# One level of Strassen's method in block 0's first product for two chunks, a new order of the weights, and a weight's sign made by ScalarE

## The chip, the core and the metric

The kernel runs on one core of a Trainium2 chip (trn2). The core has TensorE (PE; PEld is its weight load) for matmuls, VectorE (DVE), ScalarE (ACT) and GpSimd (POOL) for element-wise work, and SyncE (SP), whose queue issues most of the DMA transfers here. Matmuls read SBUF and write PSUM, which has eight banks; VectorE and ScalarE read PSUM and SBUF. The engines run side by side, each one in the order of its own queue, and wait for one another by semaphores.

The metric is the device time of one execution in microseconds. A profile is one further execution, taken apart: "span" runs from its first instruction to its last.

## What is computed

```python
kv  = einsum('bhsd,bhse->bhde', k, v)              # 8 batches, 8 heads, 576 rows, 64 columns
out = einsum('bhsd,bhde->bhse', q, kv)
x   = out / sqrt(mean(out**2, -1) + 1e-6) * g_norm # then heads side by side: 4608 x 512
h   = x @ w_in                                     # 512 x 2048
g   = maximum(0.01 * h, h)
y   = g @ w_out                                    # 2048 x 512
```

The kernel reads all inputs as they are given: `w_in` and `w_out` come as 64-bit floats, which no engine computes with, and are rounded to 32 bits on the chip.

## The kernel before

**Blocks and chunks.** The 4608 rows of `x` are cut into nine blocks of 512 (`NB`, `NT`), and the 2048 columns of `w_in` into four chunks of two halves (`h`) of two strips (`u`) of 128 columns (`NC`, `U`). Blocks 1 to 8 form both products by Strassen's method, with one level or two. Block 0 runs while the weights are still arriving, and forms them plainly, in `first_block`.

**A plain step of block 0.** For strip n = 0 to 15 an h group of four matmuls (128 rows of weight, 512 columns of `x`) fills a PSUM bank (`h_ps`, banks ha and hc in turn); ScalarE's Prelu (L1313) writes it to SBUF as `gT`. One step later an o group multiplies `gT` by the strip's two rows of `w_out` into four banks (`o_acc`: oa, oc, hb, hd), in which all sixteen strips add up. After each half step `between(n, half)` is called: it takes one step of block 1's attention (kv groups, transposes of q on VectorE, o_ps groups, the norm), where `steps` has one for that call, and lets some more weights be loaded and rounded.

**A weight.** There are 32 jobs (`w_jobs`): 16 of `w_in`, each of four DMAs of 128 KB, and 16 of `w_out`, each one DMA of 512 KB. In the list they take turns. A job's 512 KB land in one of seven homes (in `stage` and `pairs`, `raw_homes`), so job j + 7 can only be loaded when job j has been read. SP's queue also carries the loads of k, v and q for blocks 1 and 2 at fixed places between the jobs. `round_f64` turns 64 bits into 32: ScalarE reads the low word (`add`, L264) and the high word (`cut`, L262) into temporaries; VectorE clamps `cut` (L266), shifts it left by three (L271), sets the sign bit from it (L273) and adds the two (L278). Where the job's home is in two pieces (`w2_1`, "apart"), shift and sign go to a third temporary (`high`), and the last addition is made in two. Four temporaries with two buffers each (`spare`) go round. All these steps are pinned in program order on their engines.

**Strassen's method, one level.** `strassen(tags, left, right, done)` runs seven products in the order 1, 2, 6, 5, 7, 3, 4 (`ORDER`). A product is four matmuls of 256 columns: two of 128 rows each for two pieces of the result. Products 1, 6, 7, 4 add up in the first bank of `tags`, 2, 5, 3 in the second; 1, 2 and 5 start a bank afresh. After a product `done` is called. In `product_h`, for one chunk of h, it copies the banks after products 1, 5 and 6 to SBUF (ScalarE, L904 and its like), adds the bank to such a copy after 2, 3 and 7 (VectorE, `add`, L669) with a Prelu behind it (`relu`, L864), and after 4 takes a Prelu straight from the bank. Sums of quarters of the weights come from `sides_w1` (GpSimd, into the homes `pair(0)` and `pair(1)`), sums of quarters of `x` from `sides_x` (VectorE).

**Behind block 0.** VectorE and ScalarE copy the four `o_acc` banks to `o_all`, and ScalarE's queue issues the stores. Then block 1 begins: its first h group needs only `x` and the rounded weights, its third the first sums. GpSimd's sums for block 1 start during block 0, as soon as the homes in `pairs` that they are written to have been read for the last time; two one-element copies hold it there until the last weight is rounded.

A scheduler puts unpinned instructions in their place on each engine; matmuls and what is passed to `pin` keep the program's order.

Of the kernel before, what the change touches and what calls it, by code (L numbers as in the profile page):

```python
# [9 lines left out]

F32 = mybir.dt.float32
U32 = mybir.dt.uint32
I64 = mybir.dt.int64
AF = mybir.ActivationFunctionType
AX = mybir.AxisListType
ALU = mybir.AluOpType
# [8 lines left out]
def kernel(  # L25
# [91 lines left out]
    def pair(i, *shape):  # L117
        return view(pairs, i * NW, *shape)

    def matmul(*args, **kw):  # L120
        pin(nc.tensor.matmul(*args, **kw))  # L121
# [94 lines left out]
    def w2_rows(h, c, u):  # L216
        return w2_1[:, :, c, u, :] if h else w2_0[c][:, u:u + 1, :]
# [4 lines left out]
    def spare(n, name, dtype=F32):  # L222

        return gpool.tile([P, n], dtype, tag=next(spare_homes), name=name)
# [61 lines left out]
                w_jobs += [(w1_sb[h][c][:, u], w_in_e[:, :, :, f0:f0 + P]),  # L286
                           (w2_rows(h, c, u), w_out[f0:f0 + P].rearrange("p (v n) -> p v n", v=1 + h))]

    w_jobs[1:-1] = [w_jobs[i + 1 if i % 2 else i - 1] for i in range(1, len(w_jobs) - 1)]
    w_raws = {}  # L290
    halved = [j for j, (_, src) in enumerate(w_jobs) if src.shape[1:] == (2, N2)]

# [12 lines left out]
    def round_w(j):  # L305
        for _ in rounding(j):
            pass

    eps_sb = consts.tile([P, 1], F32, name="eps_sb")
    nc.vector.memset(eps_sb, EPS)  # L310
# [357 lines left out]
    def add(eng, out_, a, b_, minus=False, pinned=False):  # L668
        ins = eng.tensor_tensor(out_, a, b_, op=ALU.subtract if minus else ALU.add)  # L669
        if pinned or steady:  # L670
            pin(ins)

    def sides_w1(c):


        a11, a12 = w1_sb[0][c][:, :, :2, :], w1_sb[0][c][:, :, 2:, :]
        a21, a22 = w1_sb[1][c][:, :, :2, :], w1_sb[1][c][:, :, 2:, :]
        s12 = pair(0, U, 2, 2, P)
        sides = {1: a11, 2: a12, 4: a22, 5: s12[:, :, :, 0, :], 6: s12[:, :, :, 1, :]}
        add(nc.gpsimd, sides[5], a21, a22)  # L680
        add(nc.gpsimd, sides[6], sides[5], a11, True)

        def more():
            s34 = pair(1, U, 2, 2, P)
            sides.update({7: s34[:, :, :, 0, :], 3: s34[:, :, :, 1, :]})
            add(nc.gpsimd, sides[7], a11, a21, True)
            add(nc.gpsimd, sides[3], a12, sides[6], True)
        return sides, more

    w2_dram = [[dram.tile([P, 2, U, N2], F32, name=f"w2_{c}_{i}") for i in range(2)]  # L690
# [134 lines left out]
    def strassen(tags, left, right, done, order=ORDER, pieces=None):  # L825

        banks = {}
        for i in order:  # L830

            if i is None:
                yield
                continue
            b = tags[0 if i in (1, 6, 7, 4) else 1]
            if i in FRESH:
                banks[b] = ps_m.tile([P, 2, N2], F32, tag=b, name=f"{b[0]}_{b[1]}")
            bank = banks[b]
# [41 lines left out]
    def sums_of(c, to):  # L880

        g11, g21, g22, g12 = g_of(c)
        s1, s2, s3, s4 = (gpool.tile([P, 4, P], F32, tag=f"gs{i}", name=f"gs{i}")
                          for i in range(1, 5))
        to.update({1: g11, 2: g12, 3: s4, 4: g22, 5: s1, 6: s2, 7: s3})
        last_s4[c] = s4
        eng = nc.gpsimd if c < END - 1 else nc.vector
        if c == END - 1:
            yield
        add(eng, s1, g21, g22)  # L890
        add(eng, s2, s1, g11, True)
        if c == END - 1:
            yield
        add(eng, s3, g11, g21, True)
        add(eng, s4, g12, s2, True)

    def product_h(c, w_sides, x_sides, to):

        g11, g21, g22, g12 = g_of(c)

        def done(i, bank):

            if i == 1:
                nc.scalar.copy(g11, bank)  # L904
            elif i == 5:
                nc.scalar.copy(g22, bank)
            elif i == 2:
                add(nc.vector, g11, bank, g11, pinned=True)
                relu(g11)
            elif i == 6:  # L910
                nc.scalar.copy(g21, bank)
            elif i == 3:
                add(nc.vector, g21, bank, g21, pinned=True)
                relu(g21)
            elif i == 7:
                add(nc.vector, g22, bank, g22, pinned=True)
                relu(g22)
            else:
                relu(g12, bank)

        yield from strassen((("ha", "hc"), ("hb", "hd"))[c % 2], lambda i, part, r: w_sides[i][:, part, r, :],
                            lambda i, part, r: x_sides[i][:, r, :], done)
        yield from sums_of(c, to)

# [367 lines left out]
                nc.scalar.dma_start(to, o)  # L1292
        return finish

    def first_block(between):

        accs = [ps_m.tile([P, DM], F32, tag=t, name="o_acc") for t in ("oa", "oc", "hb", "hd")]
        x, last = xTs.pop(0), None
        for n in range(2 * NC * U + 1):
            now = last  # L1300
            if n < 2 * NC * U:
                c, h, u = n // (2 * U), n // U % 2, n % U
                h_ps = ps_m.tile([P, NT], F32, tag=("ha", "hc")[n % 2], name="h_ps")

                parts = 2 if n == 0 else 1
                for part in range(parts):
                    cols = slice(part * NT // parts, (part + 1) * NT // parts)
                    for e in range(NE):
                        matmul(h_ps[:, cols], lhsT=w1_sb[h][c][:, u, e, :],
                               rhs=x[:, e, cols], start=(e == 0 and part == 0),  # L1310
                               stop=(e == NE - 1), skip_group_check=True)
                gT = view(g_all[n // 4 % 2], n % 4 * NT, NT)
                act = nc.scalar.activation(gT, h_ps, func=AF.Prelu, alpha=SLOPE)  # L1313
                if n == 2 * NC * U - 1:
                    pin(act)
                last = (gT, w2_rows(h, c, u), n)
            if now is None:
                continue
            between(n, 0)
            for t in range(4):  # L1320
                halves = now[2] // U % 2
                for v in range(1 + halves):
                    cols = slice(v * N2, v * N2 + N2) if halves else slice(0, NT)
                    matmul(accs[t][:, cols], lhsT=now[0][:, t * P:(t + 1) * P],
                           rhs=now[1][:, v, :],
                           start=(now[2] == 0), stop=(n == 2 * NC * U), skip_group_check=True)
            between(n, 1)
        for t in range(4):
            o = o_homes[t].rearrange("p u n -> p (u n)")
            if t % 2:  # L1330
                nc.scalar.copy(o, accs[t])
            else:
                nc.vector.tensor_copy(o, accs[t])
            nc.scalar.dma_start(out[t * P:(t + 1) * P, :], o)
# [6 lines left out]
    loaded, rounded = 7, 5  # L1341

    def between(n, half):
        nonlocal loaded, rounded
        go(steps.get(2 * n + half, iter(())), 1)

        while half and rounded < min(3 * n + 8, 2 * n + 13, len(w_jobs) - (n < 11)):
            if loaded < len(w_jobs):
                load_w(loaded)
                loaded += 1  # L1350
                if loaded in (15, 19):
                    load_pair(1, (loaded - 15) // 4)
            round_w(rounded)
            rounded += 1
        if (n, half) == (12, 0):
            for p in range(2):
                load_pair(2, p)

    first_block(between)
    first_done = True  # L1360
    x_sides, _, sums, _ = sides_x(1)
    for _ in sums:
# [185 lines left out]
```

## Time and profile before

| | us |
|---|---|
| median of 3 runs | 910.97 (908.97 to 911.58) |
| the profiled execution | 909.77 |
| its span | 908.1 |
| block 0's first h group starts | 23.3 |
| block 1's first h group starts | 139.65 |
| VectorE busy, 27.3 to 54 / 54 to 81 / 81 to 108 / 108 to 140 us | 20.8 / 22.0 / 18.7 / 26.7 |
| ScalarE busy in the same stretches | 13.6 / 10.9 / 12.2 / 11.8 |
| GpSimd busy in the same stretches | 0.0 / 0.0 / 2.8 / 15.7 |
| DMA share in the same stretches | 1.06 / 0.99 / 0.98 / 0.33 |
| granted TensorE clock in them | 1.00 |

A line of the timeline has the start of a run of like instructions in us, how long it lasts, the engine, the line of the kernel, the operation, what it writes and reads, its shape and the number of instructions. A matmul of 32-bit floats is two instructions: an h group of four matmuls shows as x8. Where the engine stood idle before it, the idle time and what released it stand in brackets. The last instructions of a run overlap the next run's first, so the pace is read from start to start.

### The profile page before, as it was taken

To read this page: it belongs to the slowest core of one execution; us is meant where nothing else is said; L and a number is where in the kernel's file an instruction comes from. 1 tells how busy PE (TensorE), PEld (TensorE's weight loads), DVE (VectorE), ACT (ScalarE), POOL (GpSimd) and SP (SyncE) were. 2 spreads that over 40 slices of the span, in tenths; PEclk is the share of its full clock that TensorE was granted. 3 is DMA by queue.
4 is the path that set the end of the run, shared out by engine and by line. 5 is a ranking of instruction groups with operands and counts; after the bars stand their busy time and mean duration, and the time that the engine had idled before them with its cause. 6 is when DMAs were issued, how large, how long until landed. Compare 5 with 4: busy or idle time off the path is not lost.

```text
span 908.1 us, 19140 instructions
## 1 busy us (share of the span) xinstructions
PE 901.6 (99%) x7344; PEld 788.1 (87%) x7344; DVE 616.1 (68%) x942; ACT 330.0 (36%) x645; POOL 521.7 (57%) x672
## 2 busy tenths in 40 slices
PE   8999999999999999999999999999999999999998
PEld 4555558888998989998999999999999899999997
DVE  5877885676574768685977587666877674646453
ACT  5454523231334332434333343334242424232420
POOL 2000236977638784667647673767477847883730
PEclk9999999999999999999999999999999999999999
DMA  8999918977789679967997698958876768677831
GB/s 253 223 241 234 255 68 264 313 255 243 245 286 335 221 230 300 312 223 250 266 302 275 194 315 274 315 181 255 277 256 190 225 206 277 204 233 224 259 110 59
DMA packets 109530, 219.00 MB, mean 241 GB/s; under 512 B 11776, under 2 KB 51072, under 8 KB 109440
## 3 DMA queue, kind: packets, MB, share of 16 engines
q1 hardware_dynamic: 105504, 212.22, 76.1%
q10 hardware_dynamic: 3488, 4.39, 1.4%
q8 instruction: 58, 0.95, 0.4%
q0 software_dynamic: 448, 1.18, 0.3%
q14 instruction: 32, 0.26, 0.1%
HBM read 187.34 MB, written 30.41 MB: 240 GB/s over the span
## 4 chain that ended last, share of the span: by engine, by line
PE 97%; DMA 1%; DVE 1%; POOL 0%; ACT 0%; issue 0%; ACTq 0%; DVEq 0%; POOLq 0%
PE o_a L121 20%; PE o_c L121 16%; PE h_hc L121 10%; PE h_hd L121 10%; PE h_ha L121 10%; PE h_hb L121 9%; PE o_acc L121 6%; PE h_ps L121 6%; PE o_ps L121 3%; PE h_a L121 2%; PE h_b L121 2%; PE kv_ps L121 1%; PE h_c L121 1%; PE h_d L121 1%; DMA pairs<-in_v_dram 1%; PE o_hc L121 0%
## 5 line engine op out<-in xcount | busy, mean ns | idle before, releaser
L669 POOL TENSOR_TENSOR gs<-g 128x512 f32<-128x512 f32 x62 | 85.5, 1379 | 126.9 <-ACT g L864 65.2
L121 PE MATMUL o_a<-pairs,gs 128*128 128x256 f32 x472 | 111.9, 379 | 0.0
L669 DVE TENSOR_TENSOR o_all<-o_c,o_all 128x256 f32<-128x256 f32 (+2 forms) x124 | 69.5, 560 | 60.3 <-PE o_c L121 46.9
L669 POOL TENSOR_TENSOR w_all<-w_all 128x512 f32<-128x512 f32 x28 | 53.4, 1906 | 88.3 <-ACT w_all L1088 88.2
L864 ACT ACTIVATE g<-g 128x512 f32<-128x512 f32 x124 | 75.7, 630 | 67.8 <-DVE g L669 67.8
L669 DVE TENSOR_TENSOR g<-g,w_all 128x512 f32<-128x512 f32 (+1 forms) x84 | 89.8, 1069 | 11.7 <-POOL w_all L669 5.5
L121 PEld LDWEIGHTS o_a<-pairs,gs 128*128 128x128 f32 x472 | 85.5, 190 | 9.5 <-DVE o_all L669 0.2
L669 DVE TENSOR_TENSOR w_all<-h_ha,w_all 128x512 f32<-128x512 f32 x42 | 28.7, 684 | 55.4 <-PE h_ha L121 53.5
L1088 ACT COPY w_all<-h_hc 128x512 f32<-128x512 f32 x42 | 25.0, 596 | 106.7 <-PE h_hc L121 106.7
L121 PE MATMUL o_c<-pairs,gs 128*128 128x256 f32 x264 | 62.4, 379 | 0.0
L669 POOL TENSOR_TENSOR pairs<-w 128x512 f32<-128x512 f32 x4 | 5.3, 1330 | 98.6 <-DMA stage<-in_moe_w_out_dram 98.6
L669 DVE TENSOR_TENSOR o_all<-o_a,o_all 128x512 f32<-128x512 f32 (+1 forms) x53 | 35.5, 669 | 38.4 <-PE o_a L121 37.8
L669 DVE TENSOR_TENSOR g<-w_all 128x1024 f32<-128x1024 f32 x28 | 35.3, 1260 | 37.1 <-ACT w_all L1088 37.1
L121 PE MATMUL o_a<-w,g 128*128 128x256 f32 x248 | 58.8, 379 | 0.0
L121 PE MATMUL h_ps<-xT,w_all 128*128 128x512 f32 (+1 forms) x136 | 58.1, 571 | 0.3 <-DVE w_all L278 0.3
L121 PE MATMUL o_acc<-w,g 128*128 128x256 f32 (+1 forms) x192 | 57.7, 451 | 0.0
L121 PEld LDWEIGHTS o_acc<-w,g 128*128 128x128 f32 x192 | 36.3, 190 | 21.5 <-issue 17.2
L121 PEld LDWEIGHTS o_c<-pairs,gs 128*128 128x128 f32 x264 | 47.9, 190 | 5.3
L1088 ACT COPY w_all<-h_ha 128x512 f32<-128x512 f32 x42 | 24.8, 592 | 72.8 <-PE h_ha L121 72.8
L121 PEld LDWEIGHTS o_a<-w,g 128*128 128x128 f32 x248 | 45.0, 190 | 4.9
L121 PEld LDWEIGHTS h_ps<-xT,w_all 128*128 128x128 f32 x136 | 25.4, 190 | 26.9 <-issue 24.4
L121 PEld LDWEIGHTS h_ha<-stage,w_all 128*128 128x128 f32 x336 | 42.7, 192 | 3.0 <-issue 1.6
(287 smaller groups left out, 2405.3 us busy)
## 6 DMA issues: line engine op xcount, KB each, us to landing
w_all<-w SPq DMA_DIRECT2D x196, 448.0 KB, 4.7
pairs<-w SPq DMA_DIRECT2D x94, 256.0 KB, 4.5
w<-w SPq DMA_DIRECT2D x22, 448.0 KB, 5.9
v_in<-in_v_dram SPq DMA_DIRECT2D x29, 288.0 KB, 6.2
k_in<-in_k_dram SPq DMA_DIRECT2D x28, 288.0 KB, 6.3
q_in<-in_q_dram SPq DMA_DIRECT2D x46, 144.0 KB, 5.0
q_in<-in_q_dram SPq DMA_DIRECT2D x46, 140.0 KB, 5.4
w<-stage SPq DMA_DIRECT2D x12, 512.0 KB, 4.0
```

The lines of the kernel that those rows point to most:

```text
L121: pin(nc.tensor.matmul(*args, **kw))
L669: ins = eng.tensor_tensor(out_, a, b_, op=ALU.subtract if minus else ALU.add)
L864: nc.scalar.activation(t, t if src is None else src, func=AF.Prelu, alpha=SLOPE)
L1088: nc.scalar.copy(q[:, at], bank)
```

## The change

Chunks 2 and 3 of block 0 form h by one level of Strassen's method, through `product_h` with `first=True`; both use banks ha and hc, and the additions in `done` are then not pinned. Their sums of `x` are made by VectorE early in the block (`sides_x0`), their sums of weights by VectorE in `more` and `o_all`. All of h of a chunk is there before its o groups, which are kept in a queue (`to_add`) and taken up after products 2 and 3 of each chunk and behind the last one. The jobs are put in another order, in which the eight `w_in` jobs of chunks 2 and 3 stand together ahead of most of the `w_out` jobs. `ready(job)` loads and rounds ahead, in program order, what the next step needs. Rounding is cut in two (`begin_f64`, `end_f64`): the second half of a job is issued behind the first half of the next. The shift of L271 goes; in its place ScalarE's Prelu with a slope of 2^127 writes the sign as a whole number, and VectorE's next step shifts and joins in one.

```diff
-    w_jobs[1:-1] = [w_jobs[i + 1 if i % 2 else i - 1] for i in range(1, len(w_jobs) - 1)]
+    order = [0, 2, 1, 4, 3, 6, 5]
+    order += [8, 7, 10, 9, 12, 11, 14, 13, 16, 18, 20, 22, 15, 24, 26, 28, 30]
+    order += [i for i in range(17, 32, 2)]
...
+    def begin_f64(raw, n):
+        add, cut = spare(n, "add", U32), spare(n, "cut")
+        pin(nc.scalar.activation(add, raw[:, :, 0], func=AF.Copy, scale=2.0 ** -29))
+        pin(nc.scalar.activation(cut, raw[:, :, 1].bitcast(F32), func=AF.Copy, scale=2.0 ** -112))
+        pin(nc.vector.tensor_scalar(cut, cut, HIGH_MOST, -HIGH_MOST, op0=ALU.min, op1=ALU.max))
+        return add, cut
+
+    def end_f64(dst, add, cut, apart):
...
+        high = spare(a * n, "high").rearrange("p (a n) -> p a n", a=a) if apart else dst
+        pin(nc.scalar.activation(high.bitcast(I32), cut, func=AF.Prelu, scale=2.0 ** 60,
+                                 alpha=2.0 ** 127))
+        high, dst = high.bitcast(U32), dst.bitcast(U32)
+        pin(nc.vector.scalar_tensor_tensor(high, in0=cut.bitcast(U32), scalar=3, in1=high,
+                                           op0=ALU.logical_shift_left, op1=ALU.bitwise_or))
+        for at in range(2 if apart else 1):
+            i = slice(at, at + 1) if apart else slice(0, a)
+            pin(nc.vector.tensor_tensor(dst[:, i], high[:, i], add[:, i], op=ALU.add))
...
+            words = begin_f64(raw, dst.shape[1] * dst.shape[2])
+            end_w()
+            half_way.append((dst, *words, j in halved))
...
-    def product_h(c, w_sides, x_sides, to):
+    def product_h(c, w_sides, x_sides, to, first=False):
...
-                add(nc.vector, g11, bank, g11, pinned=True)
+                add(nc.vector, g11, bank, g11, pinned=not first)
...
-        yield from strassen((("ha", "hc"), ("hb", "hd"))[c % 2], lambda i, part, r: w_sides[i][:, part, r, :],
+        yield from strassen((("ha", "hc"), ("hb", "hd"))[0 if first else c % 2],
+                            lambda i, part, r: w_sides[i][:, part, r, :],
                             lambda i, part, r: x_sides[i][:, r, :], done)
-        yield from sums_of(c, to)
+        if not first:
+            yield from sums_of(c, to)
...
+    def sides_x0(x):
...
+        for t, a, b in ((t1, b12, b11), (t2, b22, t1), (t3, b22, b12), (t4, b21, t2)):
+            add(nc.vector, t, a, b, True, True)
+        return {1: b11, 2: b21, 3: b22, 4: t4, 5: t1, 6: t2, 7: t3}
...
+        plain_h(0)
+        for n in range(1, 2 * 2 * U):
+            plain_h(n)
+            hook()
+            if n == 3:
+                x_sides = sides_x0(x)
+            if n < 7:
+                plain_o()
+                hook()
...
+        for c in (2, 3):
+            for i in range(4):
+                ready(4 * c * U + 2 * i)
+            w_sides, rest = sides_w1(c, homes[c], nc.vector)
+            rest()
+            for at, _ in enumerate(product_h(c, w_sides, x_sides, {}, True)):
+                if at % 2:
+                    hook()
+                if at in (1, 5):
+                    plain_o()
+                    hook()
+            g11, g21, g22, g12 = g_of(c)
+            to_add.extend((4 * c + 2 * h + u,
+                           [(g11, g21, g12, g22)[2 * h + t // 2][:, 2 * u + t % 2, :] for t in range(4)])
+                          for h in range(2) for u in range(U))
+        while to_add:
+            plain_o()
+            hook()
...
+    def ready(job):
+        while place[job] >= rounded - 1 and rounded < len(w_jobs):
+            round_next()
```

More of the change, by code (lines that the diff above doesn't have):

```diff
@@ L12 @@
 U32 = mybir.dt.uint32
+I32 = mybir.dt.int32
 I64 = mybir.dt.int64
@@ L287 @@
                            (w2_rows(h, c, u), w_out[f0:f0 + P].rearrange("p (v n) -> p v n", v=1 + h))]
-    w_jobs[1:-1] = [w_jobs[i + 1 if i % 2 else i - 1] for i in range(1, len(w_jobs) - 1)]
+    order = [0, 2, 1, 4, 3, 6, 5]
+    order += [8, 7, 10, 9, 12, 11, 14, 13, 16, 18, 20, 22, 15, 24, 26, 28, 30]
+    order += [i for i in range(17, 32, 2)]
+    assert sorted(order) == list(range(len(w_jobs)))
+    place = {i: at for at, i in enumerate(order)}
+    w_jobs = [w_jobs[i] for i in order]
     w_raws = {}
@@ L307, in round_w, with end_w, round_on @@
             pass
+    def begin_f64(raw, n):
[5 more added lines that the diff above has]
+    def end_f64(dst, add, cut, apart):
+        a, n = dst.shape[1:]
+        add, cut = (t.rearrange("p (a n) -> p a n", a=a) for t in (add, cut))
+        high = spare(a * n, "high").rearrange("p (a n) -> p a n", a=a) if apart else dst
[7 more added lines that the diff above has]
+            pin(nc.vector.tensor_tensor(dst[:, i], high[:, i], add[:, i], op=ALU.add))
+    half_way = collections.deque()
+    def end_w():
+        while half_way:
+            end_f64(*half_way.popleft())
+    def round_on(j):
+        if w_in.dtype == I64:
+            raw, dst = w_raws.pop(j), w_jobs[j][0]
+            words = begin_f64(raw, dst.shape[1] * dst.shape[2])
+            end_w()
+            half_way.append((dst, *words, j in halved))
     eps_sb = consts.tile([P, 1], F32, name="eps_sb")
@@ L671, in add, with sides_w1 @@
             pin(ins)
-    def sides_w1(c):
+    def sides_w1(c, homes=None, eng=nc.gpsimd):
+        homes = homes or [pair(i, U, 2, 2, P) for i in range(2)]
         a11, a12 = w1_sb[0][c][:, :, :2, :], w1_sb[0][c][:, :, 2:, :]
         a21, a22 = w1_sb[1][c][:, :, :2, :], w1_sb[1][c][:, :, 2:, :]
-        s12 = pair(0, U, 2, 2, P)
+        s12 = homes[0]
         sides = {1: a11, 2: a12, 4: a22, 5: s12[:, :, :, 0, :], 6: s12[:, :, :, 1, :]}
-        add(nc.gpsimd, sides[5], a21, a22)
-        add(nc.gpsimd, sides[6], sides[5], a11, True)
+        add(eng, sides[5], a21, a22)
+        add(eng, sides[6], sides[5], a11, True)
         def more():
-            s34 = pair(1, U, 2, 2, P)
+            s34 = homes[1]
             sides.update({7: s34[:, :, :, 0, :], 3: s34[:, :, :, 1, :]})
-            add(nc.gpsimd, sides[7], a11, a21, True)
-            add(nc.gpsimd, sides[3], a12, sides[6], True)
+            add(eng, sides[7], a11, a21, True)
+            add(eng, sides[3], a12, sides[6], True)
         return sides, more
@@ L912, in done @@
             elif i == 3:
-                add(nc.vector, g21, bank, g21, pinned=True)
+                add(nc.vector, g21, bank, g21, pinned=not first)
                 relu(g21)
             elif i == 7:
-                add(nc.vector, g22, bank, g22, pinned=True)
+                add(nc.vector, g22, bank, g22, pinned=not first)
                 relu(g22)
@@ L1293, in store @@
         return finish
-    def first_block(between):
-        accs = [ps_m.tile([P, DM], F32, tag=t, name="o_acc") for t in ("oa", "oc", "hb", "hd")]
[L1298 to L1319, printed above, removed]
-            for t in range(4):
[L1321 to L1327, printed above, removed]
@@ new lines, in sides_x0, with first_block, plain_h, plain_o @@
+    def sides_x0(x):
+        b11, b12 = x[:, :2, :N2], x[:, :2, N2:]
+        b21, b22 = x[:, 2:, :N2], x[:, 2:, N2:]
+        t1, t2, t4 = xt1[0], xt24[0][:, 0], xt24[0][:, 1]
+        t3 = view(g_all[0], 0, 4, 6 * P)[:, 2:, 4 * P:]
+        for t, a, b in ((t1, b12, b11), (t2, b22, t1), (t3, b22, b12), (t4, b21, t2)):
+            add(nc.vector, t, a, b, True, True)
+        return {1: b11, 2: b21, 3: b22, 4: t4, 5: t1, 6: t2, 7: t3}
+    def first_block(between, ready):
+        accs = [ps_m.tile([P, DM], F32, tag=t, name="o_acc") for t in ("oa", "oc", "hb", "hd")]
+        x = xTs.pop(0)
+        to_add = collections.deque()
+        count = 0
+        def plain_h(n):
+            c, h, u = n // (2 * U), n // U % 2, n % U
+            ready(4 * c * U + 4 * h + 2 * u)
+            h_ps = ps_m.tile([P, NT], F32, tag=("ha", "hc")[n % 2], name="h_ps")
+            parts = 2 if n == 0 else 1
+            for part in range(parts):
+                cols = slice(part * NT // parts, (part + 1) * NT // parts)
+                for e in range(NE):
+                    matmul(h_ps[:, cols], lhsT=w1_sb[h][c][:, u, e, :],
+                           rhs=x[:, e, cols], start=(e == 0 and part == 0),
+                           stop=(e == NE - 1), skip_group_check=True)
+            gT = view(g_all[n // 4 % 2], n % 4 * NT, NT)
+            nc.scalar.activation(gT, h_ps, func=AF.Prelu, alpha=SLOPE)
+            to_add.append((n, [gT[:, t * P:(t + 1) * P] for t in range(4)]))
+        def plain_o():
+            nonlocal count
+            n, left = to_add.popleft()
+            c, h, u = n // (2 * U), n // U % 2, n % U
+            ready(4 * c * U + 4 * h + 2 * u + 1)
+            right = w2_rows(h, c, u)
+            count += 1
+            for t in range(4):
+                for v in range(1 + h):
+                    cols = slice(v * N2, v * N2 + N2) if h else slice(0, NT)
+                    matmul(accs[t][:, cols], lhsT=left[t], rhs=right[:, v, :],
+                           start=(count == 1), stop=(count == 2 * NC * U), skip_group_check=True)
+        calls = iter([(n, half) for n in range(1, 2 * NC * U + 1) for half in range(2)])
+        def hook():
+            call = next(calls, None)
+            if call:
+                between(*call)
+        plain_h(0)
[7 more added lines that the diff above has]
+                hook()
+        homes = {2: [more[:, 8 * i:8 * i + 8, :].rearrange("p (u r t) m -> p u r t m", u=2, r=2)
+                     for i in range(2)],
+                 3: [view(o_all, 8 * i * P, U, 2, 2, P) for i in range(2)]}
+        for c in (2, 3):
[16 more added lines that the diff above has]
+            hook()
+        for call in calls:
+            between(*call)
@@ L1343, in between @@
     def between(n, half):
-        nonlocal loaded, rounded
         go(steps.get(2 * n + half, iter(())), 1)
[L1347 to L1354, printed above, removed]
+        while half and rounded < min(3 * n + 8, 2 * n + 13, len(w_jobs)):
+            round_next()
         if (n, half) == (12, 0):
@@ L1357, in between, with round_next @@
                 load_pair(2, p)
-    first_block(between)
+    def round_next():
+        nonlocal loaded, rounded
+        if loaded < len(w_jobs):
+            load_w(loaded)
+            loaded += 1
+            if loaded in (15, 19):
+                load_pair(1, (loaded - 15) // 4)
+        round_on(rounded)
+        rounded += 1
+        if rounded == len(w_jobs):
+            end_w()
+    def ready(job):
+        while place[job] >= rounded - 1 and rounded < len(w_jobs):
+            round_next()
+    first_block(between, ready)
     first_done = True
```

## The prediction

> **What bounds the kernel now.** I read the page's head, its chain of waits, then block 0 (27 to 140 us) engine by engine in the timeline.
>
> ```profile
> span 908.1 us, 19140 instructions
> PE 901.6 (99%) x7344; PEld 788.1 (87%) x7344; DVE 616.1 (68%) x942; ACT 330.0 (36%) x645; POOL 521.7 (57%) x672
> ...
> PE 97%; DMA 1%; DVE 1%; POOL 0%; ACT 0%; issue 0%; ACTq 0%; DVEq 0%; POOLq 0%
> ```
>
> TensorE sets the end: 97% of the chain is its own work, and in block 0 one group starts where the last stops (below: start, us, engine, line, operation, out<-in). So what is taken from TensorE comes off the end, and each idle microsecond put on it goes on the end.
>
> ```profile
> 65.83 3.60 PE L121 MATMUL o_acc<-w,g 128*128 128x512 f32 x8
> 69.36 1.28 PE L121 MATMUL kv_ps<-v_in,k_in 64*64 64x64 f32 x72
> 70.57 3.70 PE L121 MATMUL h_ps<-xT,w_all 128*128 128x512 f32 x8
> 74.11 3.62 PE L121 MATMUL o_acc<-w,g 128*128 128x256 f32 x16
> 77.56 3.60 PE L121 MATMUL h_ps<-xT,w_all 128*128 128x512 f32 x8
> ```
>
> A plain h group or o group takes 3.43 to 3.45 us from start to start (77.56 - 74.11), a kv group 1.21. A group of a Strassen product (4 matmuls of 256 columns) is in the chain of waits of block 1:
>
> ```profile
> 152.38 1.73 PE h_a L121 x8
> 154.10 1.73 PE h_b L121 x8
> ```
>
> The other three engines round the weights meanwhile. One weight on VectorE (clamp, shift, or, add), and its two passes on ScalarE behind a Prelu of h:
>
> ```profile
> 85.21 0.42 DVE L266 TENSOR_SCALAR cut<-cut 128x512 f32<-128x512 f32 x1
> 85.66 0.43 DVE L271 TENSOR_SCALAR w_all<-cut 128x512 uint32<-128x512 uint32 x1
> 86.12 0.69 DVE L273 SCALAR_TENSOR_TENSOR w_all<-cut,w_all 128x512 uint32<-128x512 uint32 x1
> 86.85 0.69 DVE L278 CUSTOM_DVE_ANT_0 w_all<-w_all,add 128x1024 uint16<-128x1024 uint16 x1
> ...
> 88.08 0.60 ACT L1313 ACTIVATE g<-h_ps 128x512 f32<-128x512 f32 x1 [4.03 <-PE h_ps L121]
> 88.57 0.67 ACT L264 ACTIVATE add<-stage 128x512 uint32<-128x512 uint32 x1
> 89.13 0.67 ACT L262 ACTIVATE cut<-stage 128x512 f32<-128x512 f32 x1
> ```
>
> From start to start: clamp 0.46 where the next instruction reads it (0.33 where not: 48.84 to 49.17), shift 0.46, or 0.72, add 0.61; a ScalarE pass 0.57. While GpSimd's first additions run (105.02 to 107.93), VectorE's own stretch:
>
> ```profile
> 105.43 1.38 DVE L271 TENSOR_SCALAR w<-cut 128x512 uint32<-128x512 uint32 x1
> 106.84 1.64 DVE L273 SCALAR_TENSOR_TENSOR w<-cut,w 128x512 uint32<-128x512 uint32 x1
> ```
>
> **What the change takes off TensorE.** Eight plain h groups (chunks 2 and 3) at 3.433: 27.5 us. It adds 14 products at 1.727: 24.2 us. **-3.3 us.** The o groups stay 16 of 3.45.
>
> **Edits that cost nothing of themselves.** The new order moves the same bytes over SP's queue: a weight of four 128 KB loads and one of a single 512 KB load each land about 2.3 us after the last, and the DMA share is 0.98 to 1.06 up to 108 us. Products 1 and 2 of chunk 2 start at 74.0 on weights that in the trace are ready by 74; product 6 wants its weight sum at 74.0 + 2 x 1.73 + 3.45 (an o group) = 80.9, the eighteenth-place weight is added at 76.24 to 76.93, and four sums (0.60 + 0.60 + 0.72 + 0.72 = 2.6) end at about 79.6: the cover is 1.3 us, and without it the price is 0 to 2. VectorE loses 27 shifts (27 x 0.46 = 12.4 us) and gains 4 sums of x, 8 of weights and 6 additions from PSUM (18 at 0.6 to 0.7 = 12 us): even. ScalarE gains 27 sign passes and 6 copies or Prelus (33 x 0.57 = 19 us) and was a third to a half busy. The trace has no Prelu from SBUF to whole numbers; the nearest rows are a copy to uint32 (0.57) and L864's Prelu within SBUF (0.63 long, 0.54 apart): 0.54 to 0.69, and I take 0.57. So no engine runs out of time on average; the question is where they wait for each other.
>
> **Where it adds waits.** In the built order VectorE's and ScalarE's queues mix rounding with the Strassen steps. VectorE's additions of products 7 and 3 of chunk 2 stand ahead of the rounding of four weights (places 20 to 23), these ahead of chunk 3's four weight sums, two transposes of q, the copies of kv and the addition of chunk 3's product 2, and only then the last two steps of the weight that the first o group within chunk 3 multiplies by. Time 0 is the end of product 3 of chunk 2:
>
> - ScalarE: held by product 7's addition until -0.9; then two Prelus and four weights of three passes, 14 x 0.57 = 8.0: ends at 7.2, seen at 7.3.
> - VectorE: or + add of that weight 1.45, sums 2.64, transposes 1.10 twice and kv copies 0.39, a clamp 0.33, product 2's addition 0.60, or + add of the o weight 1.45: 9.1. It is ready at **16.4**.
> - TensorE in the same time: o group 3.45, kv 1.21, product 4 1.73, a wait of 0.85 (chunk 3's product 1 refills the bank that product 4 has just left: 0.20 from the last matmul to ScalarE, 0.60 for its Prelu, 0.05 back), products 1 and 2 3.45: **10.7**.
>
> So TensorE waits 16.4 - 10.7 = 5.7 us ahead of that o group, besides the 0.85. Who is late next: product 7 of chunk 3 needs ScalarE's copy of product 6, which stands behind the passes of all remaining weights. These come at VectorE's pace, 0.33 + 0.72 + 0.64 = 1.70 a weight: 16.4 + 4 x 1.70 + one ScalarE weight 1.7 + the copy 0.65 = 25.6, while TensorE is there at 16.4 + 3.45 + 2 x 1.73 + 0.9 (o_ps) = 24.2: **1.4 us** more. Behind it, six o groups (20.7 us) lie ready and cover the rest, and from block 1 on the instructions are the same and TensorE has no slack to take a delay up.
>
> GpSimd's first four additions can start as soon as ScalarE has read the weights of places 26 and 27, which now falls in just this stretch. In the trace they lengthen four VectorE instructions by 0.95, 0.95, 1.05 and 1.06, 4.0 us. On the path that is 0 (they fall beside waits) to 4.0; I take **2.0**, as some of VectorE's work here reads PSUM or is the add, which no row shows stretched. [...]
>
> **Sum:** -3.3 + 0.85 + 5.7 + 1.4 + 2.0 = +6.65 us. The profiled execution took 909.77 us (span 908.1 and 1.7 around it) and would be 916.4; it lies 1.2 under the median of the runs, 910.97, so on that scale **917.6**. Bounds: sign passes at 0.54 to 0.69 change 14 + 6 passes by -0.6 to +2.4; GpSimd -2.0 to +2.0; product 6's cover 0 to +2: about 914.5 to 922.
>
> **Rivals.**
> 1. *The saving is delivered (faster).* Place: the first o group within chunk 3. If VectorE's queue from product 3 to that weight takes under 10.7 us and not 16.4, TensorE waits there for nothing: 910.97 - 3.3 + 0.85 = 908.5, and 907.7 if the bank is free in time too. For: over 27 to 140 us VectorE idles 16.4 us ahead of clamps, so rounding could be well ahead by then. Against: that idling cannot be used where the queue is in order and the additions of products 7 and 3 stand in front.
> 2. *Half of it.* The queue is shorter by some 4 us (rounding ahead by two weights), GpSimd's additions fall elsewhere: -3.3 + 0.85 + 1.7 + 1.4 = +0.65: 911.6. For: the transposes may find time earlier. Against: the built order puts them behind the sums.
> 3. *The clock.* TensorE's first matmuls of 512 columns start 0.85 us apart (four in 1.54 to 5.35) and the later ones 0.43, so it begins at half clock for some 4.6 us; at the end the window view grants 1.00 up to 907.2 us and 0.53 after it, 2.7 us after the last matmul (904.5). A wait of 5.7 us may do the same: 4.6 us at half pace lose 2.3. If the copy behind product 6 were late anyway, it hides 1.4 of it; else 919.9. [...]
> 4. *Supply.* With two weights of four loads in flight and not three, the loads fall behind; each 1 us of lateness at the 18th place costs up to 1 us once the cover of 1.3 is used. Against: the DMA share is already 1. It would give 919 to 923.
>
> That the products are not what the diff says is excluded by the built order, which lists them.
>
> **Chances.** The forecast 0.60, the clock 0.13, supply or worse 0.04, half of it 0.13 (0.10 of it within 0.3% of before), the saving delivered 0.10 (0.07 of it beyond 0.3%). 0.3%, 2.7 us, is about what a measurement of this kernel can tell from no change. So faster 0.07, same 0.13, slower 0.80. The range 912.0 to 922.0 leaves out the saving, part of the half case and the worst supply, under 2 in 10; the forecast's own is 914.5 to 922.
>
> **What would show it.** Fourteen groups of 1.73 us in 74 to 120 us; an idle TensorE ahead of the o_acc group between products 2 and 6 of the second seven, released by VectorE's add of a w_out weight; a shorter one ahead of their product 7, released by ScalarE; one of 0.8 between the two chunks. Block 1's first h_a group (139.65 before) at about 146. It is wrong if that group starts before 141, or if TensorE's waits sum to under 5 us.

## The result, and the profile after

The changed kernel takes 916.97 us (median of 5 runs, 916.28 to 920.66) where the kernel before, on the same chip, takes 910.15 (5 runs, 908.97 to 911.58): a ratio of 1.0089, 95% interval 1.0062 to 1.0115. It is slower, by 0.9%. The forecast was 917.6, worked out from the first three runs of the kernel before (910.97); from 910.15 the same sum gives 916.8. The profiled execution after took 916.28 us, the one before 909.77.

The head of the page after, and its chain of waits:

```profile
span 914.6 us, 19247 instructions
PE 900.4 (98%) x7392; PEld 797.2 (87%) x7392; DVE 614.4 (67%) x933; ACT 347.9 (38%) x678; POOL 521.8 (57%) x672
...
PE 88%; DMA 8%; ACT 2%; DVE 1%; issue 0%; POOL 0%; SPq 0%; ACTq 0%; POOLq 0%
```

TensorE's busy time hardly moved (901.6 before), the span grew by 6.5 us, and TensorE's own share of the chain fell from 97% to 88%: the chain now runs back through other engines' work and the loads that fed it. The 8% of DMA is not by itself a sign of a late load: the chain passes to a load of k at 98.81 us, where VectorE had no idle time (its addition before ran to 98.88). TensorE in block 0, in the timeline:

```profile
87.70 3.62 PE L122 MATMUL o_acc<-w,g 128*128 128x256 f32 x16
...
92.45 1.99 PE L122 MATMUL h_a<-xt,w_all 128*128 128x256 f32 x8
95.30 1.99 PE L122 MATMUL h_a<-xT,w_all 128*128 128x256 f32 x8 [0.86 <-ACT g L908]
...
104.78 5.44 PE L122 MATMUL o_acc<-w,g 128*128 128x512 f32 x8 [5.76 <-DVE w L336]
110.06 1.89 PE L122 MATMUL h_a<-xt,o_all 128*128 128x256 f32 x8
...
115.91 1.99 PE L122 MATMUL h_a<-g,o_all 128*128 128x256 f32 x8 [1.32 <-ACT g L955]
...
146.59 1.89 PE L122 MATMUL h_a<-xT,w_all 128*128 128x256 f32 x8
```

The three waits that were forecast stand where they were forecast: 0.86 us between product 4 of chunk 2 (92.45) and product 1 of chunk 3 (95.30), 5.76 ahead of the o group within chunk 3, 1.32 ahead of its product 7. And one thing more: that o group lasts 5.28 us from start to start (104.78 to 110.06), not 3.43. The windows view says why (us, busy time and number of instructions of PE, PEld, DVE, ACT and POOL, then the granted clock, the DMA share and GB/s):

```profile
101.00:103.00 2.00, 0.00 (x0) 0.00 (x0) 2.00 (x4) 0.64 (x2) 1.92 (x2) 0.62 0.91 251
105.00:107.00 2.00, 2.00 (x3) 0.95 (x4) 1.97 (x3) 1.19 (x2) 2.00 (x2) 0.50 1.04 274
```

The clock fell to one half within the wait (by the trace's clock record at 101.49 us, back at 108.32), and the o group ran the first 3.54 of its 5.28 us at that pace.

The account, over the same stretch of work (from the first instruction that differs on TensorE, 74.11 before and 73.62 after, to block 1's first h_a group, 139.65 and 146.59): 65.54 us before, 72.97 after, **+7.43**. Waits 0.86 + 5.76 + 1.32 = 7.94; the half clock 5.28 - 3.43 = 1.85; the rest, 72.97 - 7.94 - 1.85 = 63.18, is 2.36 under before, which is the 3.3 saved less some 0.9 in short gaps of 0.1 to 0.2 us between groups (0.18 ahead of 80.71, 0.10 ahead of 113.61 and 0.19 ahead of 119.73 among them). The changed kernel reaches the stretch 0.49 us sooner (73.62 against 74.11), and from block 1's start to the end of the span both take about the same (768.4 before, 768.0 after): 7.43 - 0.49 - 0.4 is the 6.5 by which the span grew. Nothing behind block 0 takes the delay up, and nothing adds to it.

On VectorE, some steps of the first o weight within chunk 3 and of the one after it; and on ScalarE, the copy that product 7 waits for (start, us, engine, line, operation, out<-in):

```profile
101.35 0.97 DVE L319 TENSOR_SCALAR cut<-cut 128x512 f32<-128x512 f32 x1
102.25 0.68 DVE L712 TENSOR_TENSOR g<-h_c,g 128x512 f32<-128x512 f32 x1
102.85 1.15 DVE L332 SCALAR_TENSOR_TENSOR w<-cut,w 128x512 uint32<-128x512 uint32 x1
...
104.98 1.77 DVE L332 SCALAR_TENSOR_TENSOR w<-cut,w 128x512 uint32<-128x512 uint32 x1
106.78 1.64 DVE L336 CUSTOM_DVE_ANT_0 w<-w,add 128x1024 uint16<-128x1024 uint16 x1
...
115.30 0.56 ACT L955 COPY g<-h_a 128x512 f32<-128x512 f32 x1
```

Four instructions, 0.42 and 0.69 us at other times (110.07, 110.40 and 104.04), take 0.97, 1.15, 1.77 and 1.64, 3.0 us more in all, while GpSimd's first four additions run (100.78 to 107.87). The copy at 115.30 is for product 6, which had ended by 111.95: it stood 3.3 us behind passes of weights.

### The profile page after: what moved, and what is told of

It is laid out like the page before. It is cut to its first block, busy times and chain, and to the rows that moved or that the text cites. A ratio compares the mean times of both kernels' runs of the same rounds, so it can differ in the third digit from the quotient of the medians.

```text
span 914.6 us, 19247 instructions
## 1 busy us (share of the span) xinstructions
PE 900.4 (98%) x7392; PEld 797.2 (87%) x7392; DVE 614.4 (67%) x933; ACT 347.9 (38%) x678; POOL 521.8 (57%) x672
## 4 chain that ended last, share of the span: by engine, by line
PE 88%; DMA 8%; ACT 2%; DVE 1%; issue 0%; POOL 0%; SPq 0%; ACTq 0%; POOLq 0%
PE o_a L122 20%; PE o_c L122 16%; PE h_hc L122 10%; PE h_hd L122 10%; PE h_ha L122 10%; PE h_hb L122 9%; PE o_ps L122 3%; PE o_acc L122 3%; PE h_a L122 2%; DMA stage<-in_moe_w_in_dram 2%; PE h_b L122 2%; DMA pairs<-in_moe_w_out_dram 2%; PE h_c L122 1%; DMA pairs<-in_moe_w_in_dram 1%; PE h_d L122 1%; DMA v_in<-in_v_dram 1%
## 5 line engine op out<-in xcount | busy, mean ns | idle before, releaser
L908 ACT ACTIVATE g<-g 128x512 f32<-128x512 f32 x130 | 79.5, 631 | 71.1 <-DVE g L712 71.1
L122 PE MATMUL h_ha<-stage,w_all 128*128 128x128 f32 x336 | 44.9, 277 | 0.0
L122 PE MATMUL h_hc<-stage,w_all 128*128 128x128 f32 x336 | 44.9, 276 | 0.0
```

The costliest lines, as they stand in the source:

```text
L908: nc.scalar.activation(t, t if src is None else src, func=AF.Prelu, alpha=SLOPE)
```

## The experiments

Ten kernels. A stretch is, as above, from TensorE's first instruction that differs to block 1's first h_a group; the ratio is to the kernel before on the same chip, whose median was 909.45 us for e1 to e4, 909.59 for e5 to e8 and 909.54 for e9 and e10.

| | median us | ratio, 95% interval | stretch us | waits in it over 0.25 us |
|---|---|---|---|---|
| before | 910.15 | | 65.54 | none |
| after | 916.97 | 1.0089 (1.0062 to 1.0115) | 72.97 | 0.86, 5.76, 1.32 |
| e1 rounding alone | 911.12 | 1.0015 (1.0006 to 1.0024) | 66.40 | 0.58 |
| e2 products alone | 914.93 | 1.0068 (1.0055 to 1.0081) | 70.08 | 1.46 (load), 0.69, 3.71 |
| e3 GpSimd held | 914.93 | 1.0058 (1.0046 to 1.0070) | 71.65 | 0.85, 4.71 |
| e4 kept busy | 920.44 | 1.0120 (1.0100 to 1.0140) | 75.88 | 0.90, 1.48, 3.06 |
| e5 o weight earlier | 918.20 | 1.0091 (1.0078 to 1.0104) | 73.61 | 0.69, 7.11, 0.68 |
| e6 paced | 908.27 | 0.9987 (0.9977 to 0.9997) | 62.92 | none |
| e7 paced, o weight earlier still | 907.20 | 0.9976 (0.9966 to 0.9985) | 63.39 | 0.90 |
| e8 paced, old order | 915.34 | 1.0064 (1.0052 to 1.0076) | 71.40 | 6.82 |
| e9 paced, old rounding | 915.55 | 1.0050 (1.0028 to 1.0073) | 67.15 | 0.28, 2.4 (load) |
| e10 paced, half behind | 912.40 | 1.0022 (1.0004 to 1.0039) | 69.75 | 0.6 (load), 3.23 |

**e1 and e2: the two parts, each alone.** e1 is the kernel before with the rounding in two halves and ScalarE's sign:

```diff
-            round_w(rounded)
+            round_on(rounded)
             rounded += 1
+            if rounded == len(w_jobs):
+                end_w()
```

> The kernel before, plain block 0 and old order of the weights, with only the new rounding: cut in two and the sign made by ScalarE. Theory (the waits come from the Strassen steps and the rounding standing in one queue, so rounding alone finds nothing to hold up): block 1's first h_a group stays near 139.7 us and the time within 0.3% of the kernel before. Rival (the third ScalarE pass and the lag of one weight are dear of themselves): the first o groups wait for weights and block 1 starts 2 us or more later, 0.2% or more on the time.

Block 1 starts at 140.96, the stretch is 0.86 us longer than before, 0.58 of it one wait for ScalarE's Prelu ahead of an o group. The time is 0.15% over before: within the 0.3%, though not nothing. The rounding alone is not the cause.

e2 is the changed kernel with the rounding of before:

```diff
-            words = begin_f64(raw, dst.shape[1] * dst.shape[2])
-            end_w()
-            half_way.append((dst, *words, j in halved))
+            round_w(j)
```

> The changed kernel with the old rounding: whole, in program order, sign by VectorE; Strassen's products and the new order of the weights stay. Theory A (the wait ahead of the o group within chunk 3 comes as much from the new rounding, in which a weight's last steps stand behind the next weight's first pass and behind what lies between, as from the products): that wait falls from 5.76 us to about 1, waits of 2 to 4 us on ScalarE's copies ahead of products 5, 7 and the o_ps groups remain, block 1 starts at about 143.4 and the time is some 3 us under the changed kernel (913.5 to 914.5, where before is 910.2 and the change 917.0). Theory B (the products and the order alone put VectorE's queue late, whatever the rounding): the wait stays at 5 us or more and the time within 1 us of the changed kernel's.

```profile
101.63 3.60 PE L122 MATMUL o_acc<-w,g 128*128 128x512 f32 x8
...
115.22 1.99 PE L122 MATMUL h_c<-xT,o_all 128*128 128x256 f32 x8 [3.71 <-ACT g L947]
...
114.61 0.56 ACT L947 COPY g<-h_c 128x512 f32<-128x512 f32 x1
```

These are lines of e2, two of TensorE and one of ScalarE. The wait ahead of the o group is gone, and 3.71 us ahead of product 3 of chunk 3 remain: product 3 adds to the bank in which product 5 stands, and ScalarE's copy of it, at 114.61, stood behind passes of weights. Theory A had such waits, but ahead of products 5 and 7 and of the o_ps groups; of these only the second o_ps group lost time, 1.1 us (it takes 1.99 us from start to start and not 0.92). The time is 2.0 us under the changed kernel's, not 3. The size is not clean: a late v_in load held TensorE 1.46 us ahead of a kv group at 94 us, which gave VectorE as much time. The o group's weight was done at 100.46, 1.17 us ahead of the group, so without the late load a wait of 0.3 at most would have been left. So the o group's wait needs both parts: the products' steps in VectorE's queue, and a weight whose last two steps lag behind the next weight's first ones.

**e3: GpSimd's additions held.**

```diff
+    for t in (t12, t34):
+        nc.gpsimd.tensor_copy(t[:1, 0, 0, :1], w2_1[:1, 1, NC - 1, U - 1, :1])
     h_sides, more_h = sides_w1(0)
```

> The changed kernel with GpSimd's first four additions held back, by two more one-element copies, until the last weight is rounded. Theory (the five VectorE instructions at 101 to 108 us that took 0.97, 1.15, 1.77, 1.64 us and the like instead of 0.42 and 0.69 were stretched by those additions, and lie on the path): each takes its plain time, the wait ahead of the o group falls from 5.76 to 4.8 to 5.1 us, the copy ahead of product 7 comes some 2 us earlier, block 1 starts at 143.4 to 144.6 and the time falls by 2.0 to 2.7 us against the changed kernel. Rival (the stretches fall beside waits): block 1 stays within 0.5 us of 146.59. Loss: the additions come later and block 1 may wait for their sums; then its start moves and the time doesn't.

```profile
103.70 6.75 PE L122 MATMUL o_acc<-w,g 128*128 128x512 f32 x8 [4.71 <-DVE w L336]
110.28 1.89 PE L122 MATMUL h_a<-xt,o_all 128*128 128x256 f32 x8
...
145.25 1.89 PE L122 MATMUL h_a<-xT,w_all 128*128 128x256 f32 x8
```

The wait fell by 1.05 and the one ahead of product 7 went, 2.37 us in all: the stretched instructions were on the path. But the o group now takes 6.58 us and not 5.28, since all but its last 0.4 us lie within the half clock (103.03 to 109.86 in this trace), so 1.30 of it is given back; with a few shorter gaps the stretch is 1.32 shorter. The time fell by 2.0 us, as expected; block 1 starts at 145.25, later than the 143.4 to 144.6 expected, which had left the clock out.

**e4: TensorE kept busy in the wait.**

```diff
+                if at == 1 and c == 3:
+                    for t in (0, 1, 2, 3, 0):
+                        matmul(accs[t], lhsT=x[:, t, :P], rhs=group[:, NP:NP + 1].to_broadcast([P, NT]),
+                               start=False, stop=False, skip_group_check=True)
                 if at in (1, 5):
                     plain_o()
```

> The changed kernel with five more matmuls of 128 by 512 on zeros, which add nothing to the o banks, in the wait ahead of the o group between products 2 and 6 of chunk 3 (4.3 us of TensorE's time at full clock). It leaves VectorE's and ScalarE's work as it is. Theory (the clock at one half from 101.49 to 108.32 us cost the o group 1.85 us, but ScalarE's copy ahead of product 7 is late anyway and hides it): the clock is 1.0 throughout, the o group takes 3.43 and not 5.28 us, the wait ahead of product 7 grows from 1.32 to about 3.2, block 1 starts within 0.4 us of 146.59 and the time stays within 1 us of the changed kernel's. Rival (the lost clock is on the path): block 1 starts at about 144.7 and the time falls by 1.9 us. Other rival (an idle TensorE doesn't lower the clock): the clock falls all the same.

```profile
99.06 4.47 PE L122 MATMUL o_acc<-group,xT 128*128 128x512 f32 x10
105.01 3.70 PE L122 MATMUL o_acc<-w,g 128*128 128x512 f32 x8 [1.48 <-DVE w L336]
...
116.14 3.78 PE L122 MATMUL h_a<-g,o_all 128*128 128x256 f32 x8 [3.06 <-ACT g L955]
119.71 3.16 PE L122 MATMUL h_c<-xT,o_all 128*128 128x256 f32 x8
```

Neither theory foresaw this. The o group is back at 3.53 us and the wait ahead of product 7 grew to 3.06, as expected of a loss that ScalarE hid. But then the clock fell in that wait (115.44 to 122.27): products 7 and 3 take 3.57 and 3.09 us from start to start (the next group starts at 122.80) where the changed kernel's take 1.90 and 1.92, and behind them nothing waits, so 2.8 us go onto the path (the stretch grew by 2.91). The lost 1.85 of the changed kernel was hidden, and by filling one wait the loss was moved to where it counts.

**e5: the late weight alone moved forward.**

```diff
-    order += [8, 7, 10, 9, 12, 11, 14, 13, 16, 18, 20, 22, 15, 24, 26, 28, 30]
-    order += [i for i in range(17, 32, 2)]
+    order += [8, 7, 10, 9, 12, 11, 14, 13, 16, 18, 20, 22, 15, 24, 17, 26, 28, 30,
+              19, 21, 23, 25, 27, 29, 31]
```

> The changed kernel with one thing moved: the w_out weight that the first o group within chunk 3 multiplies by is loaded and rounded two places earlier (behind one of chunk 3's four w_in weights, not behind all four). Theory (VectorE's queue is late as a whole, so a weight moved forward puts back what was in front of it): the wait of 5.76 us ahead of the o group is gone, and one of 4 to 6 us on VectorE's weight sums stands ahead of product 6 of chunk 3, with the clock at one half behind it; block 1 starts at 144 to 147 and the time is 3 us to 0 under the changed kernel's. Rival (that weight alone is late): the wait goes and none takes its place, block 1 starts at about 141 and the time is 911 to 912.

```profile
98.89 3.60 PE L122 MATMUL o_acc<-w,g 128*128 128x512 f32 x8
109.61 3.49 PE L122 MATMUL h_a<-xt,o_all 128*128 128x256 f32 x8 [7.11 <-DVE o_all L711]
```

The o group follows product 2 at once, and product 6 waits 7.11 us for the weight sums that the moved weight pushed back. Block 1 starts at 147.44 and the time is 918.2 us: the wait is longer than the 4 to 6 us expected, and nothing was gained, where 0 to 3 us had been expected. The rival falls: not one weight is late, VectorE's queue is.

**e6, e7 and e8: both queues paced by hand.** e6 takes e5's order and adds (`cap` bounds the hooks' rounding, 25 at first):

```diff
+            if c == 3:
+                pace(27)
             w_sides, rest = sides_w1(c, homes[c], nc.vector)
...
+                if c == 3 and at == 3:
+                    pace(99)
...
+    def pace(n):
+        nonlocal cap
+        cap = n
+        while n == 99 and rounded < len(w_jobs):
+            round_next()
...
-        while place[job] >= rounded - 1 and rounded < len(w_jobs):
+        while place[job] >= rounded:
             round_next()
+        if place[job] == rounded - 1:
+            end_w()
```

and gives chunk 3 its two banks the other way round. e7 has the weight (job 17) one place further forward, e8 e6's pace with the changed kernel's order.

> The changed kernel with the order of e5, and the rounding paced by hand: 25 weights at most are begun ahead of chunk 3 and 27 ahead of the end of its product 5, the rest in one go there, so that ScalarE's copies behind products 6 and 5 stand ahead of the passes of the last weights; the second half of a weight that is needed next is issued at once and not behind the next weight's first half; and chunk 3 takes banks hc and ha the other way round, so that its product 1 finds a free bank. Products, o groups, sums, the new rounding and the bytes stay. Theory (all the lost time is a matter of what stands ahead of what in two in-order queues): no wait of more than 1 us in block 0 behind 75 us, the clock at 1.0, block 1's first h_a group at 136.0 to 138.0, and the time 1.5 to 3 us under the kernel before (907 to 909). Rival (the weights are too late, or VectorE or ScalarE has too much to do): waits of 3 us or more remain in all and block 1 starts behind 139.7.

> e6 with that w_out weight one place earlier still, ahead of all four w_in weights of chunk 3. If VectorE's queue has slack in chunk 2 (it idled 3.2 and 1.0 us there), nothing is paid for it but up to 0.9 us ahead of product 6 of chunk 2: block 1 starts at 135.9 to 137.5, within 0.5 us of e6. If the w_in weights have none, chunk 3's product 6 waits for its sums by 1.5 us or more.

> e6 with the changed kernel's own order of the weights. Theory (order and pace must both be mended, since VectorE has four weights and four sums ahead of that w_out weight): the wait ahead of the o group is 5 to 7 us, those on ScalarE's copies are gone, block 1 starts at 142.5 to 145 and the time is 913 to 916. Rival (the pace alone is the cause): that wait falls under 2 us and the time is within 1 us of e6.

TensorE's lines of e6:

```profile
93.11 1.99 PE L122 MATMUL h_a<-xt,w_all 128*128 128x256 f32 x8
94.95 1.89 PE L122 MATMUL h_c<-xT,w_all 128*128 128x256 f32 x8
...
98.40 3.60 PE L122 MATMUL o_acc<-w,g 128*128 128x512 f32 x8
...
106.70 2.00 PE L122 MATMUL h_c<-g,o_all 128*128 128x256 f32 x8
...
137.21 1.89 PE L122 MATMUL h_a<-xT,w_all 128*128 128x256 f32 x8
```

and the head of e7's page:

```profile
span 905.0 us, 19252 instructions
```

In e6 no wait over 0.2 us (0.17 ahead of product 6 of chunk 3 is the longest) is left in block 0 behind 75 us, and the clock is whole until the end. Its stretch, 62.92, is 2.62 under before; e7's, 63.39 with a wait of 0.90 in it, is 2.15 under. The medians are 1.3 and 2.4 us under the kernel before on their chip (909.59), and both intervals lie below 1. For e6 that is a little less than the 1.5 to 3 expected; its profiled execution, 909.65 us, gave most of the 2.62 back in later blocks, where TensorE waited 1.42 and 0.76 us for loads (at 283 and 577 us), which it did not in the kernel before's or e7's. e7's one wait stands ahead of product 6 of chunk 2, as expected, and block 1 starts at 136.83. So the 3.3 us of fewer matmuls are there to be had in block 0, less the short gaps, with the same products, sums, rounding and bytes: what the changed kernel lost was a matter of order alone, of the steps in the queues and of the two banks. e8 shows that the pace without the order is not enough:

```profile
104.52 5.50 PE L122 MATMUL o_acc<-w,g 128*128 128x512 f32 x8 [6.82 <-DVE w L336]
```

**e9 and e10: one edit of e6 taken back.** e9 has the old rounding (e2's edit, and the old test in `ready`), e10 only the old test in `ready`, so that a weight's second half waits for the next weight's first.

> The order, pace and banks of e6 with the old rounding: a weight whole and in program order, the sign by VectorE (27 shifts more on VectorE, 27 passes fewer on ScalarE). Theory (once paced, the new rounding is worth having, since it takes 0.46 us a weight from VectorE, whose queue is the fuller one): waits of 0.4 to 0.7 us ahead of products 6 and 7 of chunk 2, 1 to 1.6 us on VectorE's sums ahead of product 6 of chunk 3, and some 2 us in block 1 where ScalarE's copy of its product 1 stands behind the stores of block 0's result, which wait for VectorE; block 1 starts at 137.5 to 139 and the time is 2 to 4 us above e6 (910 to 912). Rival (the sign pass gives nothing): within 1 us of e6.

> e6 without one of its edits: the second half of a weight goes again behind the next weight's first half, as in the changed kernel. Theory (the lag of one weight costs where the weight is needed next): a wait of 2.5 to 3.5 us on VectorE's sums ahead of product 6 of chunk 3, block 1 at 138.7 to 140 or, if the clock falls in that wait, up to 143; the time 2 to 3 us above e6. Rival (the lag is hidden): within 0.7 us of e6.

```profile
95.89 3.34 PE L122 MATMUL h_a<-xt,w_all 128*128 128x256 f32 x8
...
148.80 2.73 PE L122 MATMUL h_a<-xt,pairs 128*128 128x256 f32 x8 [3.66 <-issue]
```

That is e9: its median is 7.3 us above e6's, which was taken on another chip; about twice what was expected. The wait in block 1 came (3.66 us, put down to "issue"): ScalarE's copy of product 1 starts at 148.11, behind two stores that held its queue from 141.9 to 145.5. The profile puts that down to another transfer, and not to VectorE, whose copies had ended at 141.45. The sums made TensorE wait for nothing, but a v_in load did, by 2.4 us, and the clock fell in both places. Whether the old rounding makes the loads late or memory was slower there is open: from 20 to 50 us e9's execution moved 205 to 220 GB/s, e10's on the same chip, with the new rounding, 214 to 225, e2's 193 to 213, after's 227 to 249. All eight runs of e9 took 914.3 to 916.1 us, so it was no accident of one execution. So the direction of the theory is borne out, its size is not settled.

```profile
105.90 3.75 PE L122 MATMUL h_c<-xt,o_all 128*128 128x256 f32 x8 [3.23 <-DVE o_all L711]
109.45 2.96 PE L122 MATMUL h_a<-xt,o_all 128*128 128x256 f32 x8
```

That is e10: 3.23 us on the sums ahead of product 6, as expected, then products 6 and 5 at half clock (3.55 and 2.88 us from start to start, the second up to an o_ps group at 112.33). The lag of one weight costs what the theory said, and the clock the rest: the median is 4.1 us above e6's (2 to 3 expected), and block 1 starts at 143.75 in this execution, which at 914.93 us was the slowest of twelve.

## Why the prediction was right, point by point

- *The products, -3.3.* A group takes 1.73 us (73.62 to 75.35). Net of all waits the work shrank by 2.36 in the changed kernel and by 2.62 in e6; the short gaps that the new groups bring, 0.7 to 0.9 us, were in no term.
- *The bank, +0.85.* Measured 0.86, and gone with the banks turned round (e6).
- *The o group within chunk 3, +5.7.* Measured 5.76. VectorE was ready 17.1 us behind the end of product 3 of chunk 2 (87.70 to 104.78) and not 16.4, TensorE at 11.3 and not 10.7. Of VectorE's 17.1, 1.05 is GpSimd's doing (e3), which the prediction had in another term; without it the queue was 0.3 us shorter than worked out. The mechanism holds against its rivals: the weight alone moved (e5) only moves the wait, the pace alone leaves it (e8), and order and pace together, with a needed weight's second half issued at once, remove it (e6, e10).
- *Product 7, +1.4, and GpSimd, +2.0.* Measured 1.32 for the one, and for the other nothing that can be read alone. The copy came 28.2 us behind product 3 and not 25.6, since GpSimd's additions stretched VectorE by 3.0 us, which the 25.6 did not have (2.0 stood in a term of its own, and the add step, 0.69 to 1.64, had been taken as untouched). TensorE came 26.9 us behind and not 24.2, since the clock fell (1.85) and the o group began 0.7 later. That 1.32 is so near 1.4 is luck: both sides came 2.6 to 2.7 later. Together the three make 5.76 + 1.85 + 1.32 = 8.93, forecast 5.7 + 1.4 + 2.0 = 9.1, with the clock, which the sum did not have, in the place of most of the 2.0. Without the additions the stretch is 1.32 us shorter, not 2.0 (e3).
- *The clock as a rival.* It did fall in the 5.7 us wait, which the forecast did not have, and cost that o group 1.85 us (2.3 in the rival); its condition, that the late copy hides it, held in full, because the copy was 2.6 us later than worked out. That the loss lay off the path is shown by e4 and e3 together: with the o group at full pace (e4) product 7 waits 1.74 longer, and with the copy early (e3) the half clock costs 3.15 and all of it counts.
- *Edits at no cost.* Rounding and sign by ScalarE: 0.15% alone (e1), 0.86 us of it in the stretch, where the forecast had nothing. In the changed kernel the new rounding's lag is part of the wait of 5.76, which the working had: with the old rounding (e2) the time is 2.0 us lower. ScalarE's busy time rose by 17.9 us (forecast 19), VectorE's fell by 1.7 (forecast even). A sign pass takes 0.62 us, 0.52 from start to start (0.57 taken). Product 6 of chunk 2 found its sum (it starts at 80.71, right behind the o group), but the cover of 1.3 us was used up: that sum ended at 80.57, and all four at 81.29 where 79.6 had been worked out.
- *The saving delivered, and supply.* The first is false of this kernel and true of e6: there VectorE rounds one weight at 85.13 to 87.06 us, in chunk 2, where it idled for 3.21 us in the changed kernel (ahead of 86.24), and the o group's weight is done at 93.00, ahead of the sums. Supply is excluded: the weights of places 20 to 24 had landed by 79.5 us, while ScalarE read place 21 at 87.50, behind the Prelu that waited for product 7.
- *The range.* The bounds that the prediction names add up to 915.0 to 924.0 and not to 914.5 to 922; 916.97 lies within both.

## What to carry to other kernels

A saving on the engine that sets the end is paid out only if the in-order queues that feed it still deliver; before making the step, list what stands ahead of each instruction that the shortened engine will wait for, and move whole sequences, since moving one item forward puts the wait on the next. Work that another engine can do at any time (here the rounding of the last weights) must be paced behind the few steps that free a bank or hand on a result. And a wait of a few microseconds can be dearer than it looks: in these runs the clock fell in or just behind waits of 2.39 us (e9) to 7.11 us (e5), and cost the o group of the changed kernel 1.85 us. Filling one wait did not help here, since another stood behind it (e4).

## What the runs showed of the hardware

**In these traces the clock changed at multiples of 3.413 us, and fell where TensorE had worked little.** Every stretch of the trace's clock records between two changes is a whole multiple of 3.413 us (half clock for 6.827 in six traces and for 3.413 twice in e9; full clock for 88.747 to 109.226 ahead of it, 95.573 in the changed kernel; for 901.119 in the kernel before). Laying windows of that length from the first change, and adding up TensorE's busy time in each (worked out from the trace's instructions):

```
window at full clock, busy share   what followed
after 98.1 us      0.28            half
e3    99.6         0.00            half
e4   112.0         0.31            half
e5   102.5         0.01            half
e8    97.9         0.00            half
e9    91.8, 146.4  0.30, 0.31      half
e10  101.4         0.38            half
e2   110.0, 113.4  0.44, 0.47      full: its wait of 3.71 us lies across two windows
window at half clock
e10  104.8         0.67            half for another window
e3, e4             0.80            half for another window
e5   109.3         0.90            full
```

So in these windows the clock fell behind a busy share of 0.38 or less and not behind 0.44, and came back behind 0.90 and not behind 0.80; what decides in between, no run shows. The length of a wait alone doesn't tell it: the clock fell with 3.06 us of waiting in e4, behind an o_ps group that filled little of the window (0.31), and with 2.39 us in e9 (0.30), while with 3.71 us in e2 it did not (0.44 and 0.47). The times of one kernel spread with it: of e10's twelve runs, the three with a mean clock of 1.000 took 909.4 to 911.0 us, the six at 0.998 took 911.4 to 913.4, and the three at 0.996 took 914.6 to 914.9. The kernel before isn't free of it: on that chip two of its 19 runs, at a mean clock of 0.998 and 0.996, took 915.4 and 916.6 us.

**GpSimd's additions stretched VectorE's custom addition too** (L336, 0.69 to 1.64 us), which reads two operands from SBUF; the stretches in the changed kernel are 0.46, 0.55, 0.95 and 1.08 us beside additions of 1.27 to 1.71 us. The sizes go with when the addition ends: the four end 0.3 us (the clamp) or 0.55 us (the other three) behind an addition's end (102.05, 103.46, 106.20 and 107.87 us), and the first two stretched instructions of the kernel before, at 105.43 and 106.84, 0.3 and 0.55 us behind theirs (106.53 and 107.93). So each of the six stretches is some 0.15 us less than what was left of the addition when the instruction began (1.08 of 1.22 at 104.98, 0.46 of 0.61 at 102.85); a clamp that began 0.15 us ahead of an addition (104.64) took its plain 0.42. The addition that reads PSUM (102.25, 0.68 us) was not stretched, with GpSimd's second addition running beside it (102.13 to 103.46).
